# Key and probability transposes moved from PE to DVE's 32x32 blocks, with 512-column output projections, in a one-core decode kernel

## The chip, the cores and the metric

The kernel runs on one core of a Trainium2 chip. A core has five engines that run side by side and meet through semaphores: PE (matrix products), DVE (vector), ACT (activations), POOL, and SP, which here only issues transfers. Data moves from HBM into SBUF (128 partitions) by 16 DMA engines; PE writes into PSUM, 8 banks of 512 words per partition, and DVE or ACT read it out.

The metric is the device time of the program in microseconds: the median of 3 runs before is 231.6 us (231.56 to 231.65).

## The reference

One decode step for two batch rows: layer norm of x, grouped-query attention over the last 4096 positions of a cache (32 query heads, 8 key heads of 128 channels), and a gated MLP, both added to x.

```python
W = min(4096, max(256, Sk // 4))                      # 4096
q = (x @ wq).reshape(B, Sq, Hq, Dh).transpose(0, 2, 1, 3)
k = jnp.repeat(k_cache[:, :, Sk - W:, :], rep, axis=1)
v = jnp.repeat(v_cache[:, :, Sk - W:, :], rep, axis=1)
p = _softmax(jnp.einsum("bhqd,bhkd->bhqk", q, k) * (Dh ** -0.5))
o = jnp.einsum("bhqk,bhkd->bhqd", p, v)               # ... @ wo
...
gate = xn @ W_gate; gate = gate * (gate > 0)
mlp = (gate * (xn @ W_up)) @ W_down
return x + attention(xn) + mlp                        # all float32
```

## The kernel before

**Tiles.** The 16 (batch row, key head) pairs are worked on in `NG` = 4 groups `g`, each one batch row and `C` = 4 key heads, and each group in `NP` = 2 steps `a` of two heads. A step loads one key tile and later one value tile of [128, 8192] words (4 MiB): partition `2 * pk + h` holds 64 successive positions of head `h` of the two. All big loads (wq in two, w_gate, w_up, 8 key tiles, 8 value tiles, w_down, wo in two) go through one pool `ring` of four buffers and one queue, SP's, in program order. A load can be issued when the buffer four loads back has been read for the last time; SP stands at it until then, and so do the loads behind it.

**Keys.** The scores need keys with channels on the partitions. In `transposes` (L305 to L316) PE turns a key tile 128x128 at a time into a PSUM bank `pk`, and DVE and ACT by turns copy each bank into `kT`, separating the two heads. `kT` (two buffers) holds half a tile (`s1` = 0 or 1), 2 heads of 2048 positions. `scores` (L329) multiplies it with `qz`, in which each head's four queries stand in columns of their own: 8 products of 512 columns per half, whose outputs go to the four groups `32 * q` of 32 rows of the bank `s`.

**Softmax.** `softmax` takes the maxima over each row (`m`), turns them (`mt`), joins the rows of one query (`mx`, `mb`), turns them back (`nm`), and one ACT instruction writes the exponentials `p`, each twice. PE turns `p` in 8 pieces (`pp`), and DVE copies with a mask `own` into `pt`.

**Values.** `values` multiplies `pt` with a value tile, 16 products on four row groups of `o`; `o` is copied to `on`, and `gather` adds up the parts that belong to a head into `oa` by four small products. `finish` divides by the sums, `spread_heads` puts the heads where wo needs them (`oT`).

**Order.** The kernel is written with a manual schedule: each engine executes in the order of the program text. `kwork` weaves: the generator `softmax(g - 1)` is advanced by one piece after each bank of transposes of group `g`, and the scores of a half tile follow the transposes of the next half. `values` of group `g - 1` come after the transposes of the same step of `g`.

**Ends.** Ahead of the loop stand the norm, q (`q_ps`, `qt`, `qz`) and the MLP's two products (`g_ps`, `u_ps`, `x_ps`, `ht_ps`). Behind it `project` multiplies each of the 49 rows of 512 of w_down and wo in four products of 128 columns (`y_ps`, 17 output rows on each of the four groups); wo's second half is loaded in parts of 8, 5, 2 and 1 of its 16 rows, and the output leaves when the last part has been used.

Of the kernel before, what the change touches and what calls it, by code (L numbers as in the profile page):

```python
# [20 lines left out]
def kernel(  # L21
# [28 lines left out]
    S1 = W // (Q * 512)  # L50

# [10 lines left out]
    ps_kt = ctx.enter_context(tc.tile_pool(name="ps_kt", bufs=3, space=PSUM))  # L62
# [77 lines left out]

    NSLOT = C * S1
# [21 lines left out]
    for e in range(NE):  # L163
# [3 lines left out]
    pick = const.tile([P, 4, 24], F32, name="pick")  # L167
    nc.gpsimd.memset(pick, 0.0)
    nc.vector.tensor_reduce(
        out=pick[:, :, 8:16], in_=ident.rearrange("p (q u k) -> p u k q", q=Q, u=4), op=ALU.add, axis=AX.X  # L170
    )


    HK = 2 * REP
    by_h = const.tile([P, NP, HK], F32, name="by_h")
    nc.vector.tensor_reduce(
        out=by_h, in_=ident.rearrange("p (q a s k) -> p a k q s", q=Q, a=NP, s=S1), op=ALU.add, axis=AX.XY
    )

    half_of = const.tile([P, 2], F32, name="half_of")  # L180
    nc.vector.tensor_reduce(
        out=half_of, in_=ident.rearrange("p (y h) -> p h y", h=2), op=ALU.add, axis=AX.X
    )
    own = const.tile([P, 2, REP], F32, name="own")
    nc.vector.tensor_copy(own, half_of[:, :, None].to_broadcast([P, 2, REP]))
# [42 lines left out]
    for r in range(R):  # L228
        qs = work.tile([P, 512], F32, name=f"qs{r}", tag="qs")
        (nc.vector.tensor_copy if r else nc.scalar.copy)(qs, q_ps[r])  # L230
        qt = ps_kt.tile([P, REP, C, 16, B], F32, name=f"qt{r}", tag="kt")
        for i in range(REP):
            nc.tensor.transpose(
                qt[:, i].rearrange("p c s b -> p (c s b)"), qs[:, i * P:(i + 1) * P], ident
            )
        for b in range(B):
            dst = qz[:, r * B + b].rearrange("p (a s h k) -> p a s h k", a=NP, s=S1, h=2)
            for h in range(2):
                nc.vector.tensor_copy(
                    dst[:, :, :, h, 0:REP], qt[:, :, h::2, 0:S1, b].rearrange("p i a s -> p a s i")  # L240
                )
# [4 lines left out]
    x_ps = ps_1.tile([32, 2, FX], F32, name="x_ps", tag="o0")  # L246
# [36 lines left out]
    ht_ps = ps_1.tile([P, FM + SX, B], F32, name="ht_ps", tag="misc")  # L283
    for k in range(FM):
        for c in range(Q):
            nc.tensor.matmul(
                ht_ps[32 * c:32 * c + 32, k], hh[:, k], ident[:, 32 * c:32 * c + B], start=True, stop=True
            )
    for k in range(SX):
        m = 64 if k < RX else 32  # L290
        nc.tensor.matmul(ht_ps[0:m, FM + k], hx[:, k, 0:m], ident[0:32, 0:B], start=True, stop=True)
    nc.vector.tensor_copy(hT[:, 0:FM, :, 0], ht_ps[:, 0:FM])
    nc.vector.tensor_copy(hT[0:64, FM:FM + RX, :, 0], ht_ps[0:64, FM:FM + RX])
    if LEFT:
        nc.vector.tensor_copy(hT[0:32, FM + RX, :, 0], ht_ps[0:32, FM + RX])

    HW = W // S1
    ss, pts, rls = {}, {}, {}  # L300
    kts, osb = {}, {}
    turn = [0]

    def evacuate(dst, src):
        (nc.vector.tensor_copy if turn[0] % 2 else nc.scalar.copy)(dst, src)  # L305
        turn[0] += 1

    def transposes(g, a, s1, kt_in):

        kt = ktp.tile([P, 2, HW], F32, name=f"kT{g}_{a}_{s1}", tag="kT")  # L310
        kts[g, a, s1] = kt
        for n in range(2 * Q):
            pk = ps_kt.tile([P, 512], F32, name=f"pk{g}_{a}_{s1}_{n}", tag="kt")
            for u in range(4):
                j = 8 * Q * s1 + 4 * n + u
                nc.tensor.transpose(pk[:, u * P:(u + 1) * P], kt_in[:, j * P:(j + 1) * P], ident)  # L316
            evacuate(
                kt[:, :, n * 256:(n + 1) * 256], pk.rearrange("p (y h) -> p h y", h=2),
            )
            yield  # L320

    def scores(g, a, s1):
        if (a, s1) == (0, 0):
            ss[g] = ps_s.tile([P, 512], F32, name=f"s{g}", tag="s")
        kt = kts.pop((g, a, s1))
        for h in range(2):
            n = (a * S1 + s1) * 2 + h
            for q in range(Q):
                nc.tensor.matmul(  # L329
                    ss[g][32 * q:32 * q + 32, :], qz[:, g, 32 * n:32 * n + 32],  # L330
                    kt[:, h, q * 512:(q + 1) * 512],
                    start=(a == 0 and s1 == 0 and h == 0), stop=(a == NP - 1 and s1 == S1 - 1 and h == 1),
                )

    def softmax(g):
# [3 lines left out]
        yield  # L339
        mt = ps_1.tile([1, P], F32, name=f"mt{g}", tag="misc")  # L340
        nc.tensor.transpose(mt, m, ident)
        mx = work.tile([1, NP, HK], F32, name=f"mx{g}", tag="mx")
        nc.vector.tensor_reduce(
            out=mx, in_=mt.rearrange("p (q a s k) -> p a k q s", q=Q, a=NP, s=S1), op=ALU.max, axis=AX.XY
        )
        mb = work.tile([1, NP, S1, HK], F32, name=f"mb{g}", tag="mb")
        nc.vector.tensor_scalar(
            mb, mx[:, :, None, :].to_broadcast([1, NP, S1, HK]), -SCALE, None, op0=ALU.mult
        )
        yield  # L350
        nm_ps = ps_1.tile([P, 1], F32, name=f"nm_ps{g}", tag="misc")
        for q in range(Q):
            nc.tensor.matmul(
                nm_ps[32 * q:32 * q + 32, :], mb.rearrange("p a s k -> p (a s k)"), ones, start=True, stop=True
            )
        nm = work.tile([P, 1], F32, name=f"nm{g}", tag="nm")
        nc.vector.tensor_copy(nm, nm_ps)  # L357

        p = work.tile([P, 512, 2], F32, name=f"p{g}", tag="p", bufs=1)
        l = work.tile([P, 1], F32, name=f"l{g}", tag="l")  # L360
        both = ss[g][:, :, None].to_broadcast([P, 512, 2])
        nc.scalar.activation(p, both, AF.Exp, bias=nm, scale=SCALE, accum_out=l)  # L362
        yield
        yield
        yield

        pts[g] = work.tile([P, 2, Q * NP * S1, 4, HK], F32, name=f"pt{g}", tag="pt")
        pv = p.rearrange("r y h -> r (y h)")
        for jh in range(2):
            pp = ps_kt.tile([P, 4, P], F32, name=f"pp{g}_{jh}", tag="kt")  # L370
            for u in range(4):
                lo = (4 * jh + u) * P
                nc.tensor.transpose(pp[:, u], pv[:, lo:lo + P], ident)  # L373
            nc.vector.tensor_tensor(  # L374
                pts[g][:, jh].rearrange("p n u k -> p u n k"), pp.rearrange("p u (n k) -> p u n k", k=HK),
# [56 lines left out]
    def kwork(g, a, kt_in, others=()):  # L432
# [11 lines left out]
        for o in others:  # L444
            for _ in o:
                pass
# [85 lines left out]
```

## Time and profile before

| | |
|---|---|
| median of 3 runs | 231.60 us |
| the profiled execution | 231.43 us, of which its span is 229.6 us |
| PE busy | 185.4 us (mean granted clock 0.938) |
| DVE busy | 67.2 us |
| ACT busy | 46.9 us |
| DMA | 94.90 MB read, queue busy 96.7% of the span |

The span runs from the first instruction of the program on the core to the last; what lies around it, 1.8 us here, is start and end of the execution. Busy times of PE are of pipelined products and overlap; a line `x256` counts records, two for each float32 product. In the groups of instructions the first number behind the bar is the busy time of all, then the mean duration of one in ns, then the idle time before them and who ended it. In the windows PEclk is the granted PE clock as a share of the full one, and the DMA share is the mean busy share of the 16 DMA engines.

### The profile page before, as it was taken

The numbers are of one execution on the slowest core, as the hardware profiler recorded it, in microseconds if no ns is written. First come the engines' busy times: TensorE is split into PE (matmuls) and PEld (weight loads), VectorE is DVE, ScalarE is ACT, GpSimd is POOL, SyncE is SP. The second block draws the span as 40 slices with busy tenths as digits, with TensorE's granted clock in tenths as the row PEclk, the third lists the DMA queues.
The fourth block names the chain that finished last, engine by engine and source line by source line (L and its number), as shares of the span: only waits on it lengthen the run. The fifth ranks groups of instructions, "written<-read, shape, count | busy, mean of one in ns | idle before, by whom it ended". The sixth has DMA issues, their size and how long they took to land.

```text
span 229.6 us, 4149 instructions
## 1 busy us (share of the span) xinstructions
PE 185.4 (81%) x1876; PEld 114.7 (50%) x1876; DVE 67.2 (29%) x135; ACT 46.9 (20%) x80; POOL 8.2 (4%) x25
## 2 busy tenths in 40 slices
PE   0059961779999899997799699889979973988794
PEld 0052231259666583663484566458446532247682
DVE  0320021034444570441472143157124224001000
ACT  0020100004344451440351233045023202010000
POOL 8100000000000000000000000000000300000000
PEclk9999999577999999999999799999999999599678
DMA  7999999999999999999999999999999999999981
GB/s 274 451 428 408 454 410 437 422 451 442 405 425 451 415 417 445 442 411 420 457 417 432 428 440 414 434 445 414 422 440 437 417 428 440 423 442 414 410 364 49
DMA packets 3824, 95.15 MB, mean 414 GB/s; under 512 B 434, under 2 KB 448, under 8 KB 704
## 3 DMA queue, kind: packets, MB, share of 16 engines
q1 hardware_dynamic: 3796, 94.90, 96.7%
q8 instruction: 14, 0.23, 0.4%
q14 instruction: 2, 0.02, 0.0%
q10 hardware_dynamic: 12, 0.00, 0.0%
HBM read 94.90 MB, written 0.00 MB: 413 GB/s over the span
## 4 chain that ended last, share of the span: by engine, by line
DMA 54%; PE 41%; DVE 2%; issue 1%; ACT 1%; ACTq 0%; POOL 0%; DVEq 0%
DMA k<-in_A_k_cache_dram 37%; PE pk L316 21%; DMA wo<-in_A_wo_dram 13%; PE s L329 7%; PE y_ps L480 5%; DMA x<-in_A_x_dram 4%; PE o L393 3%; PE q_ps L222 3%; PE xt_ps L212 2%; ACT p L362 1%; PE pp L373 0%; ACTq L135 0%; PE oa L409 0%; DVE stats L189 0%; DVE kT L305 0%
## 5 line engine op out<-in xcount | busy, mean ns | idle before, releaser
L316 PE MATMUL pk<-ident,k 128*128 128x128 f32 x512 | 67.9, 286 | 6.0 <-DMA k<-in_A_k_cache_dram 5.9
L316 PEld LDWEIGHTS pk<-ident,k 128*128 128x128 f32 x512 | 57.9, 146 | 20.9 <-issue 16.7
L305 DVE COPY kT<-pk 128x512 f32<-128x512 f32 x64 | 44.2, 691 | 52.1 <-PE pk L316 46.2
L305 ACT COPY kT<-pk 128x512 f32<-128x512 f32 x64 | 37.5, 585 | 69.5 <-PE pk L316 69.5
L393 PE MATMUL o<-v,pt 128*32 128x512 f32 x256 | 32.5, 641 | 0.0
L329 PE MATMUL s<-kT,qz 128*32 128x512 f32 x256 | 30.9, 598 | 0.0
L393 PEld LDWEIGHTS o<-v,pt 128*32 128x32 f32 x256 | 11.3, 117 | 15.7 <-issue 10.9
L212 PE MATMUL xt_ps<-rep,xn 2*128 2x32 f32 x16 | 3.7, 400 | 13.9 <-DVE xn L206 13.9
L329 PEld LDWEIGHTS s<-kT,qz 128*32 128x32 f32 x256 | 7.1, 109 | 11.9 <-issue 11.5
L305 DVE COPY on<-o 128x512 f32<-128x512 f32 x4 | 2.8, 692 | 30.5 <-PE o L393 30.5
L409 PE MATMUL oa<-on,pick 128*16 128x128 f32 x64 | 8.3, 273 | 4.1 <-DVE on L305 3.3
L480 PE MATMUL y_ps<-wo,oT 128*17 128x128 f32 x256 | 10.3, 329 | 1.6 <-DMA wo<-in_A_wo_dram 1.6
L409 PEld LDWEIGHTS oa<-on,pick 128*16 128x16 f32 x64 | 5.8, 97 | 11.3 <-DVE on L305 7.0
L250 PE MATMUL u_ps<-wu,xnT 128*32 128x416 f32 x32 | 5.8, 901 | 6.1 <-DMA wu<-in_B_W_up_dram 6.1
L212 PEld LDWEIGHTS xt_ps<-rep,xn 2*128 2x128 f32 x16 | 3.6, 320 | 13.9 <-issue 13.9
L222 PE MATMUL q_ps<-wq,xnT 128*32 128x512 f32 x64 | 9.7, 777 | 0.5 <-DVE xnT L214 0.5
L480 PEld LDWEIGHTS y_ps<-wo,oT 128*17 128x17 f32 x256 | 8.1, 119 | 3.6 <-DMA wo<-in_A_wo_dram 2.6
L305 ACT COPY on<-o 128x512 f32<-128x512 f32 x4 | 2.3, 586 | 27.0 <-PE o L393 27.0
L98 POOL MEMSET wx<- 64x2048 f32 x1 | 1.8, 1804 | 169.1 <-PE s L329 169.1
L362 ACT ACTIVATE p<-s,nm 128x1024 f32<-128x1024 f32 x4 | 4.5, 1114 | 13.1 <-DVE nm L357 13.1
L374 DVE TENSOR_TENSOR pt<-pp,own 128x512 f32<-128x512 f32 x8 | 5.4, 689 | 2.6 <-PE pp L373 2.6
L373 PE MATMUL pp<-ident,p 128*128 128x128 f32 x32 | 4.9, 280 | 1.7 <-ACT p L362 1.5
(83 smaller groups left out, 68.2 us busy)
## 6 DMA issues: line engine op xcount, KB each, us to landing
k<-in_A_k_cache_dram SPq DMA_DIRECT2D x8, 4096.0 KB, 23.9
v<-in_A_v_cache_dram SPq DMA_DIRECT2D x8, 4096.0 KB, 28.3
wq<-in_A_wq_dram SPq DMA_DIRECT2D x2, 4096.0 KB, 21.7
wo<-in_A_wo_dram SPq DMA_DIRECT2D x1, 4096.0 KB
wg<-in_B_W_gate_dram SPq DMA_DIRECT2D x1, 3584.0 KB, 29.8
wu<-in_B_W_up_dram SPq DMA_DIRECT2D x1, 3584.0 KB, 39.3
wd<-in_B_W_down_dram SPq DMA_DIRECT2D x1, 3328.0 KB
wo<-in_A_wo_dram SPq DMA_DIRECT2D x1, 2048.0 KB
```

The source lines that it names most:

```text
L212: nc.tensor.matmul(xt_ps[:, o, kc, :], cols, rep.rearrange("r s b -> r (s b)"), start=True, stop=True)
L222: nc.tensor.matmul(q_ps[r][32 * c:32 * c + 32, :], xnT[:, 0, kc, :], wqt[kc // 2][:, kc % 2, n * 512:(n + 1) * 512], start=(kc == 0), stop ...
L250: nc.tensor.matmul(dst[32 * c:32 * c + 32, :], xnT[:, 1, kc, :], wt[:, kc, c * MQ:(c + 1) * MQ], start=(kc == 0), stop=(kc == KC - 1),)
L305: (nc.vector.tensor_copy if turn[0] % 2 else nc.scalar.copy)(dst, src)
L316: nc.tensor.transpose(pk[:, u * P:(u + 1) * P], kt_in[:, j * P:(j + 1) * P], ident)
L329: nc.tensor.matmul(ss[g][32 * q:32 * q + 32, :], qz[:, g, 32 * n:32 * n + 32], kt[:, h, q * 512:(q + 1) * 512], start=(a == 0 and s1 == 0 ...
L362: nc.scalar.activation(p, both, AF.Exp, bias=nm, scale=SCALE, accum_out=l)
L373: nc.tensor.transpose(pp[:, u], pv[:, lo:lo + P], ident)
L374: nc.vector.tensor_tensor(pts[g][:, jh].rearrange("p n u k -> p u n k"), pp.rearrange("p u (n k) -> p u n k", k=HK), own.rearrange("p h i ...
L393: nc.tensor.matmul(o[32 * q:32 * q + 32, :], pts[g][:, jh, n].rearrange("p u k -> p (u k)"), v[:, lo:lo + 512], start=(s1 == 0 and jh == 0 ...
L409: nc.tensor.matmul(oa[g], pick[:, u, 8 - 8 * a:24 - 8 * a], ons[a][:, u], start=(a == 0 and u == 0), stop=(a == NP - 1 and u == 3),)
L480: nc.tensor.matmul(y_ps[32 * e:32 * e + 17, :], lhsT.rearrange("p b s -> p (b s)")[:, 0:17], w[:, e * P:(e + 1) * P], start=False, stop=stop,)
```

## The change

The key tile is no longer turned by PE. DVE's transpose turns each 32x32 block by itself, so channels `32 * c` to `32 * c + 31` of 32 partitions (16 runs of positions, two heads) land on 32 partitions; `kT` becomes [128, 4 channel blocks, 2 heads, 32 positions, 16 runs], and `qz` block diagonal: partition group `pb` holds q for its own positions only, with q copied to the four partition groups by products with `spot`. The two heads of a key tile are now `a` and `a + 2`.

```diff
@@ load_kv
-        base = cache[b, r * C + 2 * a, SK - W:SK, :]
+        base = cache[b, r * C + a, SK - W:SK, :]
-            tensor=cache.tensor, offset=base.offset, ap=[[run, PK], [SK * DH, 2], [1, run]]
+            tensor=cache.tensor, offset=base.offset, ap=[[run, PK], [NP * SK * DH, 2], [1, run]]
@@ set-up
-    qz = const.tile([P, NG, NSLOT * 36], F32, name="qz")
+    ZW = 3 * 16
+    qz = const.tile([P, NG, CB, 2, ZW], F32, name="qz")
     nc.gpsimd.memset(qz, 0.0)
+    spot = const.tile([P, CB, PB, L], F32, name="spot")
+    nc.gpsimd.tensor_copy(
+        spot, ident.rearrange("p (c e) -> p c e", c=CB)[:, :, None, :].to_broadcast([P, CB, PB, L])
+    )
...
+    perm = const.tile([P, 2, P], F32, name="perm")
+    nc.gpsimd.memset(perm, 0.0)
...
@@ q
+        qT = work.tile([P, B, C, REP], F32, name=f"qT{r}", tag="qT")
+        nc.vector.tensor_copy(qT, qt[:, :, :, 0, :].rearrange("p i c b -> p b c i"))
+        rq = ps_1.tile([P, CB, B, C, REP], F32, name=f"rq{r}", tag="misc")
+        for cb in range(CB):
+            nc.tensor.matmul(
+                rq[:, cb].rearrange("p b c i -> p (b c i)"), spot[:, cb].rearrange("p b e -> p (b e)"),
+                qT.rearrange("p b c i -> p (b c i)"), start=True, stop=True,
+            )
...
@@ keys
-            for u in range(4):
-                j = 8 * Q * s1 + 4 * n + u
-                nc.tensor.transpose(pk[:, u * P:(u + 1) * P], kt_in[:, j * P:(j + 1) * P], ident)
-            evacuate(
-                kt[:, :, n * 256:(n + 1) * 256], pk.rearrange("p (y h) -> p h y", h=2),
-            )
...
+        for s1 in range(S1):
+            kt = ktp.tile([P, CB, 2, JH, KL], F32, name=f"kT{g}_{a}_{s1}", tag="kT")
+            for n in range(2):
+                lo = JH // 2 * n
+                j = JH * s1 + lo
+                nc.vector.transpose(
+                    kt[:, :, :, lo:lo + JH // 2, :].rearrange("p c h j k -> p j c k h"),
+                    kt_in[:, j * DH:(j + JH // 2) * DH],
                 )
+            for cb in range(CB):
+                for h in range(2):
+                    lo = 32 * (2 * s1 + h)
+                    nc.tensor.matmul(
+                        ss[g][lo:lo + 32, :], qz[:, g, cb, h, 16 * a:16 * a + 32],
+                        kt[:, cb, h].rearrange("p j k -> p (j k)"),
+                        start=(a == 0 and cb == 0), stop=(a == NP - 1 and cb == CB - 1),
+                    )
```

The softmax keeps its steps, but writes each exponential once. `turn` permutes its rows by two products with `perm` and turns the result with one DVE transpose; the mask moves behind the value products, and `gather` is one product per step followed by a sum over `u` on DVE.

```diff
+    def turn(g, p, l):
+        pp = ps_kt.tile([P, 2, 512], F32, name=f"pp{g}", tag="kt")
+        for h in range(2):
+            nc.tensor.matmul(pp[:, h], perm[:, h], p, start=True, stop=True)
+        pts[g] = work.tile([P, NP * S1, JH, HK], F32, name=f"pt{g}", tag="pt")
+        nc.vector.transpose(pts[g].rearrange("p n j k -> p j n k"), pp.rearrange("p h y -> p y h"))
...
@@ values, gather, finish
-        evacuate(ons[a].rearrange("p u d -> p (u d)"), o)
+        nc.vector.tensor_tensor(
+            ons[a], o.rearrange("p (u d) -> p u d", u=4), mask[:, :, None].to_broadcast([P, 4, P]), op=ALU.mult
+        )
...
-        for u in range(4):
-            nc.tensor.matmul(
-                oa[g], pick[:, u, 8 - 8 * a:24 - 8 * a], ons[a][:, u],
-                start=(a == 0 and u == 0), stop=(a == NP - 1 and u == 3),
-            )
+        nc.tensor.matmul(
+            oa[g], picks[:, a].rearrange("p h a i -> p (h a i)"), ons[a], start=(a == 0), stop=(a == NP - 1)
+        )
...
+        su = work.tile([HR, P], F32, name=f"su{g}", tag="su", bufs=1)
+        nc.vector.tensor_reduce(out=su, in_=oa[g].rearrange("h u d -> h d u"), op=ALU.add, axis=AX.X)
+        nc.vector.tensor_scalar(osb[r][:, b], su, rls[g], None, op0=ALU.mult)
@@ the loop
+    for g in range(NG):
+        for a in range(NP):
             kt_in = load_kv(k_cache, "k", g, a)
+            v_in = load_kv(v_cache, "v", g - 1, a) if g else None
+            scores(g, a, kt_in)
+            nm = maxima(g) if a else None
+            if g:
+                values(g - 1, a, v_in)
+            pl = softmax(g, nm) if a else None
+            if g:
+                gather(g - 1, a)
+                if a:
+                    finish(g - 1)
+                elif g % B == 1 and g > 1:
+                    spread_heads((g - 2) // B)
             if a:
...
+                turn(g, *pl)
```

At the end the rows of w_down and the first 24 of wo are each one product of 512 columns into one of four row groups of `y4`; `y4` is copied and folded into `y_ps` by four products, and the last 8 rows of wo stay products of 128 columns.

```diff
+    def slot(lhsT, w):
+        t, i = done[0] % Q, done[0]
+        nc.tensor.matmul(
+            y4[32 * t:32 * t + 32, :], lhsT.rearrange("p b s -> p (b s)"), w, start=(i < Q), stop=(i >= EARLY - Q)
+        )
+        done[0] += 1
...
+            if (r, j) < (1, cuts[1][1]):
+                slot(oT[:, r, j], wt[:, j])
+                continue
+            if j == cuts[1][1]:
+                ys = work.tile([P, D], F32, name="ys", tag="qs")
+                nc.vector.tensor_copy(ys, y4)
+                quarters(fold[:, 0:17], ys, False)
+            quarters(oT[:, r, j].rearrange("p b s -> p (b s)")[:, 0:17], wt[:, j], (r, j) == (R - 1, NJ - 1))
```

The order on DVE moves. Before, in the second step of group 2 and the start of group 3 (`kT_1_0` and `kT_1_1` are the two halves of the step's key tile, `on_1` the copy of the value product of group 1, `kT_0_0` the first half of group 3):

```order
L305 COPY kT_1_0_1052<-pk_1_0_6_1089 128x2x256
L305 COPY kT_1_1_1109<-pk_1_1_0_1110 128x2x256
L305 COPY kT_1_1_1109<-pk_1_1_2_1122 128x2x256
L305 COPY kT_1_1_1109<-pk_1_1_4_1134 128x2x256
L305 COPY kT_1_1_1109<-pk_1_1_6_1146 128x2x256
L305 COPY on_1_1188<-o_1_1171 128x512
L418 TENSOR_SCALAR osb_873<-oa_1166,rl_994 16x128
L305 COPY kT_0_0_1199<-pk_0_0_1_1206 128x2x256
L338 TENSOR_REDUCE m_1226<-s_1020 128x1
L305 COPY kT_0_0_1199<-pk_0_0_3_1228 128x2x256
L343 TENSOR_REDUCE mx_1236<-mt_1234 1x16
```

Now DVE in the same step of group 2:

```order
L337 STREAM_TRANSPOSE kT_1_0_591<-k_1_587 128x16x4x16x2 x2
L337 STREAM_TRANSPOSE kT_1_1_602<-k_1_587 128x16x4x16x2 x2
L353 TENSOR_REDUCE m_613<-s_543 128x1
L357 TENSOR_REDUCE mx_617<-mt_615 1x16
L362 TENSOR_SCALAR mb_619<-mx_617 1x64 x2
L368 COPY nm_624<-nm_ps_622 128x1
L400 TENSOR_TENSOR on_1_643<-o_1_626,mask 128x512
L417 TENSOR_REDUCE su_649<-oa_585 16x128
L418 TENSOR_SCALAR osb_526<-su_649,rl_537 16x128
L382 STREAM_TRANSPOSE pt_655<-pp_652 128x32x4x8
L386 RECIPROCAL rl_659<-lp_657 16x1
L337 STREAM_TRANSPOSE kT_0_0_666<-k_0_661 128x16x4x16x2 x2
```

The maxima of a group stood among the next group's key copies; they now stand, with the value product's mask and the turning of `p`, between the transposes of one key tile and those of the next.

PE in the same step before, from the value products of group 1 to the first transposes and maxima of group 3's start:

```order
L329 MATMUL s_1020<-kT_1_0_1052,qz 32x512 x8
L409 MATMUL oa_1166<-on_0_1046,pick 16x128 x4
L393 MATMUL o_1_1171<-v_1_1050,pt_954 32x512 x16
L409 MATMUL oa_1166<-on_1_1188,pick 16x128 x4
L316 MATMUL pk_0_0_0_1200<-ident,k_0_1195 128x128 x4
L316 MATMUL pk_0_0_1_1206<-ident,k_0_1195 128x128 x4
L329 MATMUL s_1020<-kT_1_1_1109,qz 32x512 x8
L316 MATMUL pk_0_0_2_1220<-ident,k_0_1195 128x128 x4
```

and now:

```order
L344 MATMUL s_543<-kT_1_0_591,qz 32x512 x8
L344 MATMUL s_543<-kT_1_1_602,qz 32x512 x8
L355 MATMUL mt_615<-ident,m_613 1x128
L366 MATMUL nm_ps_622<-ones,mb_619 128x1
L395 MATMUL o_1_626<-v_1_589,pt_533 32x512 x16
L408 MATMUL oa_585<-on_1_643,picks 16x512
L380 MATMUL pp_652<-p_645,perm 128x512 x2
L384 MATMUL lp_657<-l_646,by_h 16x1
L344 MATMUL s_665<-kT_0_0_666,qz 32x512 x8
```

Scores used to be followed by transposes of the next tile; now nothing of the next tile stands on PE until its own scores.

More of the change, by code (lines that the diff above doesn't have):

```diff
@@ L50 @@
     S1 = W // (Q * 512)
+    L = 32
+    PB = P // L
+    CB = DH // L
     NP = C // 2
@@ L364, in softmax @@
[L364 to L370, printed above, removed]
-            for u in range(4):
[L372 to L375, printed above, removed]
-                own.rearrange("p h i -> p (h i)")[:, None, None, :].to_broadcast([P, 4, Q * NP * S1, HK]), op=ALU.mult,
-            )
-            yield
+        nc.scalar.activation(p, ss[g], AF.Exp, bias=nm, scale=SCALE, accum_out=l)
```

184 lines of the change are left out of this document (69 added, 115 removed).

## The prediction

> **What bounds the kernel now.** I began with the page: busy times, the slices, the chain of waits.
>
> ```profile
> span 229.6 us, 4149 instructions
> PE 185.4 (81%) x1876; PEld 114.7 (50%) x1876; DVE 67.2 (29%) x135; ACT 46.9 (20%) x80; POOL 8.2 (4%) x25
> DMA  7999999999999999999999999999999999999981
> HBM read 94.90 MB, written 0.00 MB: 413 GB/s over the span
> DMA 54%; PE 41%; DVE 2%; issue 1%; ACT 1%; ACTq 0%; POOL 0%; DVEq 0%
> ```
>
> PE looks like the bound at 81%, but the transfers are busy in every slice between the first and the last two. The view by windows, over one batch-and-row group each, says the same:
>
> ```profile
> core 0: us, PE busy (x) PEld busy (x) DVE busy (x) ACT busy (x) POOL busy (x), PEclk, DMA share, GB/s
> 90.00:129.00 39.00, 34.49 (x303) 20.73 (x294) 14.65 (x25) 11.64 (x20) 0.00 (x0) 1.00 1.00 429
> 129.00:168.00 39.00, 37.12 (x307) 24.18 (x307) 14.86 (x26) 10.47 (x18) 0.00 (x0) 0.96 1.00 430
> ```
>
> A group moves four 4 MiB tiles (16.78 MB); at 430 GB/s that is **39.0 us**. As long as compute turns a group round in 39 us, it is hidden. How much lateness the ring of four buffers forgives shows in the chain of waits:
>
> ```profile
> 24.50 26.72 DMA k<-in_A_k_cache_dram
> 100.73 28.26 DMA k<-in_A_k_cache_dram
> ```
>
> The first key tile lands at 51.22. A later one is issued 28 us before it lands, and its transfer alone takes some 10: compute may slip by about 15 us once, not in every group. The kernel is bound by HBM.
>
> **The change: the transposes.** 512 PE transposes and 128 copies go. Instead DVE runs 32 transposes, two per half tile, each of 2048 elements per partition, 8 per group. No such operation stands in the trace, so its duration T is bounded by DVE rows:
>
> ```profile
> L305 DVE COPY kT<-pk 128x512 f32<-128x512 f32 x64 | 44.2, 691 | 52.1 <-PE pk L316 46.2 <-ACT on L305 5.2
> L357 DVE COPY nm<-nm_ps 128x1 f32<-128x1 f32 x4 | 0.6, 158 | 1.8 <-PE nm_ps L353 1.8
> L206 DVE TENSOR_SCALAR xn<-xc,rs 2x512 f32<-2x512 f32 x1 | 0.5, 474 | 0.0
> L261 DVE SCALAR_TENSOR_TENSOR gr<-gs 128x416 f32<-128x416 f32 x1 | 0.6, 592 | 4.5 <-ACT gs L259 4.5
> L263 DVE TENSOR_TENSOR hh<-gr,u_ps 128x416 f32<-128x416 f32 x1 | 0.9, 872 | 11.6 <-PE u_ps L250 11.6
> L374 DVE TENSOR_TENSOR pt<-pp,own 128x512 f32<-128x512 f32 x8 | 5.4, 689 | 2.6 <-PE pp L373 2.6
> ```
>
> - One element at a time: (691 - 158)/511 = 1.043 ns each, so T = 0.158 + 2047 x 1.043 ns = **2.29 us**.
> - As fast as the quickest SBUF-to-SBUF row (xn): (474 - 158)/511 = 0.62 ns, T = 1.43 us. The lower end.
> - gr and hh both handle 416 elements. hh writes each element 32 words from the last and takes 280 ns more: 0.67 ns per element. pt writes runs of 8 neighbours and pays nothing over kT. The new kT write alternates: head 0, head 1, head 0, 512 words (2 KB) apart, so no two successive elements are neighbours. With hh's surcharge: 1.043 + 0.673 = 1.716 ns, T = **3.67 us**.
> - Twice the one-element rate, as if a 4-byte word took two passes: T = 4.43 us. The upper end.
>
> I take 3.67: of these rows, hh has the write pattern that this transpose has. The Trainium skill, Vector Engine (DVE) Microarchitecture Reference, section 5.2, has 1.71 ns per column for a destination that hops 4 KiB at every element, which hh's row here bears out. Its section 3.8 says the transpose front-end sustains one element per cycle per lane; by that alone T would be 2.29 and the sum below 231.1. No row here shows a transpose; that case is a rival.
>
> **Scores.** Each half tile still takes 8 products of 512 columns, but its output rows are now `32 * (2 * s1 + h)`: two groups of 32 PE columns where there were four.
>
> ```profile
> L329 PE MATMUL s<-kT,qz 128*32 128x512 f32 x256 | 30.9, 598 | 0.0
> L255 PE MATMUL x_ps<-wg,xnT 128*32 128x128 f32 x8 | 1.0, 272 | 0.0
> 123.44 3.62 PE L393 MATMUL o<-v,pt 128*32 128x512 f32 x32
> 195.47 6.37 PE L393 MATMUL o<-v,pt 128*32 128x512 f32 x32
> ```
>
> On four groups a 512-column record costs 30.9/256 = 0.12 us. x_ps stays in one group: 8 records of 128 columns in 1.0 us less a pipeline of 0.2 is 0.11 each, so 0.44 per 512 columns. The four groups thus overlap nearly fully, and two give 0.22 per record: 16 records, **3.6 us**, where 1.9 were (the bounds). `o` keeps four groups: 3.62. The second o row is one at half clock: 6.37.
>
> **The chain.** The old order wove softmax and copies between transposes. Now DVE runs in program order: 4 transposes, then it stands at `on` until PE has done the last scores and 16 value products; the next tile's transposes are queued behind it. So these times add. In the second tile of a group the maxima, the head sum and `turn` join. Rows for them:
>
> ```profile
> L338 DVE TENSOR_REDUCE m<-s 128x1 f32<-128x512 f32 x4 | 2.8, 691 | 4.8 <-PE s L329 4.8
> L341 PE MATMUL mt<-ident,m 128*1 128x128 f32 x4 | 1.1, 272 | 0.8 <-DVE m L338 0.8
> L343 DVE TENSOR_REDUCE mx<-mt 1x16 f32<-1x128 f32 x4 | 1.1, 272 | 0.4 <-PE mt L341 0.4
> L347 DVE TENSOR_SCALAR mb<-mx 1x32 f32<-1x32 f32 x4 | 0.7, 169 | 0.1
> L353 PE MATMUL nm_ps<-ones,mb 1*32 1x1 f32 x32 | 1.0, 172 | 2.8 <-DVE mb L347 2.8
> L362 ACT ACTIVATE p<-s,nm 128x1024 f32<-128x1024 f32 x4 | 4.5, 1114 | 13.1 <-DVE nm L357 13.1
> L382 DVE RECIPROCAL rl<-lp 16x1 f32<-16x1 f32 x4 | 0.6, 146 | 0.0
> ```
>
> - Maxima: 0.69 + 0.27 + 0.27 + 0.22 (two mb, overlapping) + 0.24 (nm_ps, 1.0 over four groups) + 0.16 = 1.85.
> - `oa`, one full-width product of 512 columns (two records of 0.44): 0.9. `pp`, two of them: 1.8; the sum over u and osb run beside it. `pt`, 1024 elements in runs of 8: 0.158 + 1.07 = 1.23. `rl`: 0.15.
> - exp has half the columns of L362, about 0.7, beside `o`.
>
> First tile: 4T + 3.6 + 3.62 + 0.69 = 4T + 7.9. Second: 4T + 3.6 + 1.85 + 3.62 + 0.69 + 0.9 + 1.8 + 1.23 + 0.15 = 4T + 13.8. Some 13 handoffs at 0.06 (s ends at 112.60, m starts at 112.67 in the timeline's two rows below): 0.8.
>
> ```profile
> 110.68 1.92 PE L329 MATMUL s<-kT,qz 128*32 128x512 f32 x16
> 112.67 0.69 DVE L338 TENSOR_REDUCE m<-s 128x1 f32<-128x512 f32 x1 [1.14 <-PE s L329]
> ```
>
> **A group costs 8T + 22.5.** At T = 3.67 that is 51.9 us against the transfers' 39.0: the bound moves to the DVE-PE chain, late by 13 us per group, more than the ring forgives. What is late next is the queue: a key buffer is freed after its transposes, so SP's load stands until then, and DMA gets gaps.
>
> Group 0 has no values: 51.2 + 8T + 3.6 + 1.85 + 0.7 (exp) + 1.8 (pp) + 1.4 (pt, rl) + 0.6 (handoffs) = 61.2 + 8T. Three groups: 24T + 67.5. The tail after the last `pt`:
>
> ```profile
> 212.74 1.97 PE L423 MATMUL op<-osb,spread 16*128 16x32 f32 x16
> L480 PE MATMUL y_ps<-wd,hT 128*17 128x128 f32 x104 | 3.2, 273 | 0.0
> L502 DVE COPY yo<-y_ps 128x128 f32<-128x128 f32 x1 | 0.3, 291 | 11.7 <-PE y_ps L480 11.7
> 227.00 0.60 SPq L503 DMA_DIRECT2D out_dram<-yo  x1
> ```
>
> Two rounds of o, on, oa (10.4), 17 slots of w_down at two records of 0.12 (4.1), op and oT (2.2), 24 slots of wo (5.8), copying y4 and folding it (0.9), 8 rows in quarters at eight records of 3.2/104 = 0.031 (2.0), yo 0.3, output to the span's end 2.6, handoffs 0.8: **29.1**. Wider products save nothing: 0.24 a row against 0.25. The last wo rows land some 18 us after `pt` (two queued tiles of about 10 us, the first issued a little before it); PE asks for them at 24.
>
> Span = 61.2 + 24T + 8T + 67.5 + 29.1 = **157.8 + 32T**, but never below the transfers' 229.6. At T = 3.67: 275.2. The profiled execution took 231.43 for its 229.6, 0.2 us under the median of 231.6; with 1.8 outside the span: **277 us**.
>
> **Costed at nothing.** More set-up on POOL (a wider qz, spot, picks, perm, at most some 4 us):
>
> ```profile
> 11.75 0.55 POOL L195 TENSOR_TENSOR sd<-ve,half 2x1 f32<-2x1 f32 x1 [5.15 <-DVE ve L193]
> 41.53 5.78 PE L250 MATMUL u_ps<-wu,xnT 128*32 128x416 f32 x32 [6.14 <-DMA wu<-in_B_W_up_dram]
> ```
>
> POOL idles 5.15 us ahead of sd. Without that cover q slips by what is over, and the first key load, issued at 24.5, waits in the queue behind wu until about 41 anyway. The longer q path (rq) hides in PE's 6.14 us before wu; uncovered it costs about 1.5 us.
>
> **PE's clock.** With PE idle for 2T at the start of each tile it will be cold:
>
> ```profile
> 125.93:129.34 3.41, 1.34 (x14) 0.38 (x7) 0.00 (x0) 0.58 (x1) 0.00 (x0) 1.00 1.02 432
> 129.34:132.76 3.42, 3.42 (x18) 3.42 (x17) 1.38 (x2) 0.73 (x2) 0.00 (x0) 0.50 0.96 412
> 132.76:136.17 3.41, 3.41 (x32) 1.87 (x30) 1.38 (x2) 1.61 (x3) 0.00 (x0) 1.00 1.01 432
> ```
>
> A window with 1.34 us of work is followed by one at 0.50, and a full one restores 1.00. The first scores of a tile would then take up to 7.2 us, inside 2T = 7.3: hidden. Were `o` cold too, 2.7 us more in each tile that has values: up to 8 x 2.7 = 22.
>
> **The rivals.**
> - A, one element per cycle (T = 2.29). For: the contiguous rows. Against: hh. The formula gives a span of 231.1, 232.9 us, but 2T = 4.6 no longer hides cold scores: up to 7.2 - 4.6 = 2.6 late in a tile, about half of that where the clock comes back in their midst, and less where the queue is ahead: 233 to 244, about 239 us. Slower still. Chance 0.17. The Trainium skill's rule of one element per cycle (Vector Engine (DVE) Microarchitecture Reference, section 3.8) would make it this case; no row shows it.
> - B, on the other side: transposes at or under 2.24 us with PE warm. From 157.8 + 32T = 229.6 the point is T = 2.24; below it the chain fits within the transfers and the time is theirs, 231.6, give or take 0.8. xn's 0.62 ns is for it, the alternating write against it. Chance 0.08; nothing in the profile favours either sign within it.
> - C, two passes (T = 4.43): 157.8 + 141.8 + 1.8 = 301 us. Only the missing row is for it. Chance 0.10.
>
> **Numbers.** Forecast (T between 3.3 and 4.1, 266 to 290 us): 0.65. Leaving out B, the quickest of A, and C: 236 to 292, about 0.8. A run of this kernel can tell 0.2% from nothing; B splits into faster 0.03, same 0.03, slower 0.02; so faster 0.03, same 0.03, slower 0.94.
>
> **What would show it.** A transpose row near 3.7 us, DVE about 145 us busy (117 of it transposes), scores at 3.6 us per half tile, DMA slices below 9 from group 1 on, SP's loads waiting for DVE. It is wrong if transposes take 2.3 us, if DMA stays full, or if PE's cold clock puts o on 6 us throughout.

## The result, and the profile after

The changed kernel is slower: a median of 281.56 us (6 runs, 278.70 to 282.69) against 231.48 us (6 runs, 231.28 to 231.65) for the kernel before. The ratio is 1.2148, with a 95% interval of 1.2093 to 1.2203. The profiled execution took 278.70 us, for a span of 276.9.

The page of the changed kernel: the span, the busy times, then the busy share of DVE, the granted clock and the transfers in 40 slices, and the shares of the chain that ended last, by engine and by line.

```profile
span 276.9 us, 2272 instructions
PE 169.2 (61%) x976; PEld 54.7 (20%) x976; DVE 148.1 (53%) x125; ACT 8.6 (3%) x28; POOL 10.2 (4%) x33
DVE  1300324699952992794379639824990497240201
PEclk9999869559897759959995797799659958999999
DMA  7999999999999906997995299799907992989930
HBM read 94.90 MB, written 0.00 MB: 343 GB/s over the span
DVE 47%; PE 35%; DMA 13%; issue 3%; ACT 0%; ACTq 0%; POOL 0%; DVEq 0%
```

Before, the transfers filled every slice and headed the chain with 54%. Now they have holes (a 0 and a 6 in slices 15 and 16, then one hole or more per group), the rate is 343 GB/s where it was 413, and DVE and PE share the chain. The bytes are the same: nothing is loaded twice, loads are issued later. Who makes them late stands in the waits of SP's queue (total us, times, longest), before and now:

```profile
SPq L70 <- PE pk L316: 83.3, 8, 13.3
```

```profile
SPq L73 <- DVE kT L337: 120.3, 7, 25.4
```

Before, too, a load stood behind the transposes that read its buffer, 83 us in all, and the transfers had no hole. Now it is 120 us, and the longest wait is 25.4 us where it was 13.3. The groups of instructions give the prices (busy us and mean ns behind the bar, then the idle time before them):

```profile
L337 DVE STREAM_TRANSPOSE kT<-k 128x2048 f32<-128x2048 f32 x32 | 115.8, 3728 | 2.3 <-DMA k<-in_A_k_cache_dram 2.3
L344 PE MATMUL s<-kT,qz 128*32 128x512 f32 x256 | 76.9, 757 | 69.1 <-DVE kT L337 69.1
L382 DVE STREAM_TRANSPOSE pt<-pp 128x1024 f32<-128x1024 f32 x4 | 5.0, 1250 | 7.0 <-PE pp L380 7.0
```

One transpose of a quarter key tile takes 3.73 us, and PE idles 69 us for them. Whether the two take turns is seen in the chain of waits (start, duration, engine, tile, line, count); here is group 1, from one group's first transposes to the next's, and a piece of group 3:

```profile
91.26 14.41 DVE kT L337 x4
105.71 2.34 PE s L344 x10
...
109.34 3.46 PE o L395 x26
...
113.43 14.51 DVE kT L337 x4
...
127.98 3.65 PE s L344 x16
...
131.65 0.70 DVE m L353
...
133.80 3.62 PE o L395 x32
...
138.18 1.03 PE oa L408 x2
139.22 1.93 PE pp L380 x4
...
141.17 1.25 DVE pt L382
...
142.46 14.41 DVE kT L337 x4
...
215.95 1.03 PE oa L408 x2
216.98 1.91 PE op L423 x16
```

Read it downwards: DVE for 14.4 us, PE for 7, DVE for 14.5, then a dozen shorter steps by turns (not all are shown), and the next tile's transposes only behind them. From 91.26 to 142.46 a group takes 51.2 us, 12 more than its transfers need. Four transposes in 14.41 us mean 3.60 to 3.63 for each, some 0.1 under the mean of a single row: successive ones overlap a little.

### The profile page after: what moved, and what is told of

Its sections match the earlier page's. It is cut to its first block, busy times and chain, and to the rows that moved or that the text cites. A ratio compares the mean times of both kernels' runs of the same rounds, so it can differ in the third digit from the quotient of the medians.

```text
span 276.9 us, 2272 instructions
## 1 busy us (share of the span) xinstructions
PE 169.2 (61%) x976; PEld 54.7 (20%) x976; DVE 148.1 (53%) x125; ACT 8.6 (3%) x28; POOL 10.2 (4%) x33
## 4 chain that ended last, share of the span: by engine, by line
DVE 47%; PE 35%; DMA 13%; issue 3%; ACT 0%; ACTq 0%; POOL 0%; DVEq 0%
DVE kT L337 40%; PE o L395 10%; DMA k<-in_A_k_cache_dram 10%; PE s L344 9%; PE y L467 4%; PE pp L380 3%; DMA x<-in_A_x_dram 3%; PE oa L408 2%; PE q_ps L240 2%; DVE pt L382 2%; DVE on L400 2%; PE op L423 1%; PE xt_ps L230 1%; DVE m L353 1%; PE y_ps L474 1%
## 5 line engine op out<-in xcount | busy, mean ns | idle before, releaser
L344 PE MATMUL s<-kT,qz 128*32 128x512 f32 x256 | 76.9, 757 | 69.1 <-DVE kT L337 69.1
L337 DVE STREAM_TRANSPOSE kT<-k 128x2048 f32<-128x2048 f32 x32 | 115.8, 3728 | 2.3 <-DMA k<-in_A_k_cache_dram 2.3
L344 PEld LDWEIGHTS s<-kT,qz 128*32 128x32 f32 x256 | 16.5, 134 | 125.4 <-DVE kT L337 80.5
L400 DVE TENSOR_TENSOR on<-o,mask 128x512 f32<-128x512 f32 x8 | 5.5, 692 | 40.4 <-PE o L395 40.4
L408 PE MATMUL oa<-on,picks 128*16 128x512 f32 x16 | 8.3, 597 | 6.5 <-DVE on L400 6.5
L380 PE MATMUL pp<-p,perm 128*128 128x512 f32 x16 | 9.2, 703 | 1.2 <-ACT p L374 1.2
L382 DVE STREAM_TRANSPOSE pt<-pp 128x1024 f32<-128x1024 f32 x4 | 5.0, 1250 | 7.0 <-PE pp L380 7.0
L267 DVE COPY qz<-rq 32x32 f32<-32x32 f32 x16 | 3.0, 187 | 7.1 <-ACT qz L267 7.1
L467 PE MATMUL y<-wo,oT 128*32 128x512 f32 x48 | 5.4, 594 | 0.0
L467 PE MATMUL y<-wd,hT 128*32 128x512 f32 x26 | 4.5, 595 | 0.0
```

What stands on the lines that cost most here:

```text
L267: (nc.vector.tensor_copy if a else nc.scalar.copy)(qz[rows, r * B + b, :, :, lo:lo + REP], rq[rows, :, b, a::NP, :])
L337: nc.vector.transpose(kt[:, :, :, lo:lo + JH // 2, :].rearrange("p c h j k -> p j c k h"), kt_in[:, j * DH:(j + JH // 2) * DH],)
L344: nc.tensor.matmul(ss[g][lo:lo + 32, :], qz[:, g, cb, h, 16 * a:16 * a + 32], kt[:, cb, h].rearrange("p j k -> p (j k)"), start=(a == 0 an ...
L380: nc.tensor.matmul(pp[:, h], perm[:, h], p, start=True, stop=True)
L382: nc.vector.transpose(pts[g].rearrange("p n j k -> p j n k"), pp.rearrange("p h y -> p y h"))
L400: nc.vector.tensor_tensor(ons[a], o.rearrange("p (u d) -> p u d", u=4), mask[:, :, None].to_broadcast([P, 4, P]), op=ALU.mult)
```

## The experiments

The theory: two properties of the change make it slow. The transposes write with a hop of 2 KB at every element, and the order makes DVE and PE take turns. The first three kernels mend one of the two each, the next two take PE's share in it, and the last four the end of the kernel and the repairs together. Medians of the kernel before on the same chips were 231.24 to 231.29 us.

**Runs of 16 neighbours.** One change in the order of the write. What a column of `kT` holds is then mixed between heads and positions; the amount of work stays the same.

```diff
-                    kt[:, :, :, lo:lo + JH // 2, :].rearrange("p c h j k -> p j c k h"),
+                    kt[:, :, :, lo:lo + JH // 2, :].rearrange("p c h j k -> p j c h k"),
```

> The changed kernel, but each key transpose writes runs of 16 neighbouring words instead of alternating between two heads 2 KB apart; kT then holds keys of both heads mixed, so the scores are not the reference's; all sizes and counts are the same. Theory (the alternating write costs 0.67 ns per element, the transpose itself runs at one element per 1.04 ns): the transpose row falls from 3.73 to about 2.3 us (pitch 3.62 to 2.2), and the span by 32 x 1.4 = 45 us to 231.5, plus up to 1.4 us of cold scores in each of 8 tiles: 232 to 243 us. Rival (a transpose of 4-byte words out of SBUF costs 1.7 ns per element wherever it writes): row stays 3.7, time 279 to 283.

Measured: 240.28 us (one run), a span of 238.5. The groups of instructions of this kernel:

```profile
L337 DVE STREAM_TRANSPOSE kT<-k 128x2048 f32<-128x2048 f32 x32 | 71.0, 2272 | 3.9 <-DMA k<-in_A_k_cache_dram 2.4 <-PE s L344 1.5
```

Down from 3728 to 2272 ns: 1.11 ns for each of 2048 elements in place of 1.82. The alternating write alone cost 0.71 ns per element, and 41 of the 50 us by which the change is slower go with it. The quick price is the prediction's rival A (2.29 us), whose 239 us came out at 240.3.

**The same, with scores that are right.** The two heads alternate inside `kT`, so that the transpose writes 32 neighbours in a row, and PE reads its moving operand at a step of two words.

```diff
-            kt = ktp.tile([P, CB, 2, JH, KL], F32, name=f"kT{g}_{a}_{s1}", tag="kT")
+            kt = ktp.tile([P, CB, JH, KL, 2], F32, name=f"kT{g}_{a}_{s1}", tag="kT")
...
-                    kt[:, :, :, lo:lo + JH // 2, :].rearrange("p c h j k -> p j c k h"),
+                    kt[:, :, lo:lo + JH // 2].rearrange("p c j k h -> p j c k h"),
...
-                        kt[:, cb, h].rearrange("p j k -> p (j k)"),
+                        kt[:, cb, :, :, h].rearrange("p j k -> p (j k)"),
```

> The changed kernel with the two heads innermost in kT, so that a transpose writes 32 neighbouring words, and PE reads each head's keys in steps of two words; the result is the reference's. Theory: transposes as in the run with runs of 16 (about 2.3 us). If PE reads steps of two words at its full rate, time 232 to 245 us. Rival (PE's moving operand slows down at a step of two words): scores of a half tile take about 7.2 us instead of 3.63, PE becomes the bound within a tile, two half tiles 14.4 + o 3.6 + handoffs, 255 to 275 us.

Measured: 240.63 us (4 runs, 240.28 to 243.28), 1.0431 times the kernel before (1.0375 to 1.0487). From its page, the chain that ended last by engine, and two groups of instructions:

```profile
PE 58%; DVE 22%; DMA 15%; issue 3%; ACT 0%; ACTq 0%; POOL 0%; DVEq 0%
...
L344 PE MATMUL s<-kT,qz 128*32 128x512 f32 x256 | 65.7, 731 | 38.6 <-DVE kT L337 38.6
L337 DVE STREAM_TRANSPOSE kT<-k 128x2048 f32<-128x2048 f32 x32 | 71.0, 2272 | 3.9 <-DMA k<-in_A_k_cache_dram 2.3 <-PE s L344 1.6
```

Runs of 32 cost what runs of 16 do, and the scores take 65.7 us as in the kernel above (65.6). PE reads every second word at nearly the same rate: the 32 records of a tile's scores, after the same 3.38 us of idling, take 8.18 us against 8.04. But the repair is not whole. The chain has gone over to PE, from 35% to 58%, and the time stays 9 us over the kernel before.

**The order alone.** The alternating write stays. The transposes become a function of their own; those of the next tile's first half are written right behind the scores, those of its second half behind the softmax, ahead of `gather`, `finish` and `turn`. The maxima move behind the value products.

```diff
+    kt_in = load_kv(k_cache, "k", 0, 0)
+    kts = [keys(0, 0, s1, kt_in) for s1 in range(S1)]
...
-            scores(g, a, kt_in)
-            nm = maxima(g) if a else None
+            scores(g, a, kts)
+            gn, an = divmod(NP * g + a + 1, NP)
+            if gn < NG:
+                kt_in = load_kv(k_cache, "k", gn, an)
+                kts = [keys(gn, an, 0, kt_in)]
...
+            nm = maxima(g) if a else None
             pl = softmax(g, nm) if a else None
+            if gn < NG:
+                kts.append(keys(gn, an, 1, kt_in))
```

> The changed kernel with the same instructions in another order: the two transposes of each half of the next key tile are written ahead of on and of turn, so that DVE works on the next tile while PE does the last scores and the value products. Theory (what makes the group slow is that 8T and 22.5 us of PE round trips add up): T stays 3.7, but a group costs DVE's own 8 x 3.62 + about 6 = 35 us, less than the 39 us of its transfers, so the kernel is bound by HBM again: 231 to 238 us. Rival (DVE's or PE's own throughput is the bound, and order does not matter): at least 265 us.

Measured: 232.59 us (4 runs, 232.07 to 232.85), 1.0054 times the kernel before (1.0037 to 1.0070). From its page, the span, DVE and the transfers by slices, and the group of the transposes:

```profile
span 230.9 us, 2278 instructions
DVE  2120032259999997899998999998999804312001
DMA  7999999999999999999999999999999999999970
...
L334 DVE STREAM_TRANSPOSE kT<-k 128x2048 f32<-128x2048 f32 x32 | 117.6, 3773 | 2.9 <-DMA k<-in_A_k_cache_dram 1.8 <-PE s L347 1.1
```

The transposes are as slow as in the changed kernel, DVE is as busy (147.6 us), and yet 49 of the 50 us are gone. DVE's slices are now nearly full from slice 10 to 31 and the transfers have no hole. They are only just ahead: the chain that ended last still runs through DVE for 42% of the span and through transfers for 23%. The timeline shows DVE turning keys while PE multiplies:

```profile
93.90 5.12 PE L347 MATMUL s<-kT,qz 128*32 128x512 f32 x25
...
96.30 1.21 DVE L385 STREAM_TRANSPOSE pt<-pp 128x1024 f32<-128x1024 f32 x1
...
98.60 7.49 DVE L334 STREAM_TRANSPOSE kT<-k 128x2048 f32<-128x2048 f32 x2 [1.07 <-PE s L347]
...
99.74 4.00 PE L398 MATMUL o<-v,pt 128*32 128x512 f32 x26
```

So the two repairs overlap: 41 and 49 us, of 50 in all. Slow transposes count mostly because PE's work stands in line with them, and the line counts mostly because the transposes are slow. Neither is the whole: with runs of 32 the line still costs 9.5 us (240.63 against 231.09 us, the last kernel below). Either repair brings a group near its 39 us of transfers, and below that there is little to gain.

**Scores on four column groups.** The prediction charged 1.7 us per half tile for two groups in place of four. Here both halves of a tile add into the same four groups of rows, so the scores are sums of two halves.

```diff
-                    lo = 32 * (2 * s1 + h)
+                    lo = 32 * (2 * (cb % 2) + h)
...
-                        start=(a == 0 and cb == 0), stop=(a == NP - 1 and cb == CB - 1),
+                        start=(a == 0 and s1 == 0 and cb < 2), stop=(a == NP - 1 and s1 == S1 - 1 and cb >= 2),
```

> The changed kernel with the scores of a half tile spread over four groups of 32 output rows by the channel block's parity instead of two; both halves' scores add up in the same rows, so the result is not the reference's; all sizes and counts are the same. Theory (two groups overlap half as well as four): 16 records of a half tile fall from 3.63 to about 1.9 us, 8 tiles save 1.7 us each, 14 us in all: 263 to 268 us. Rival (the score product is limited by something else, its operands or weight loads): no change, 278 to 283 us.

Measured: 287.41 us (one run), slower than the changed kernel by more than its runs differ among themselves. Theory and rival both missed. The page's clock by slices, then the timeline of one tile:

```profile
PEclk9999669667755578655675795558667755599999
```

```profile
128.50 3.64 PE L344 MATMUL s<-kT,qz 128*32 128x512 f32 x16 [3.57 <-DVE kT L337]
...
134.59 6.38 PE L395 MATMUL o<-v,pt 128*32 128x512 f32 x32
```

And the view by windows over these two, whose columns are those of the prediction's windows:

```profile
128.50:132.14 3.64, 3.64 (x16) 0.59 (x16) 0.00 (x0) 0.00 (x0) 0.00 (x0) 0.50 0.80 288
134.59:140.97 6.38, 6.38 (x33) 1.39 (x32) 0.16 (x1) 0.78 (x2) 0.00 (x0) 0.56 0.76 329
```

The mean clock is 0.731, against 0.852. The last scores of this tile need 3.64 us, as long as on two groups in the changed kernel, and the value products 6.38 where they took 3.62. Both ran at about half the clock, 0.50 and 0.56. The scores do so throughout: the 16 records take 3.35 to 3.64 us in each of the 16 half tiles. The reading is that PE now works too little to be granted the full clock; it idles 3.57 us ahead of these scores, where it was 1.61. To tell this from four groups that are simply no faster, PE got the missing work back.

**Four groups, the first half's products twice.** Each product of a tile's first half is issued twice, so the scores count that half double.

```diff
-            for cb in range(CB):
+            for i, cb in enumerate(list(range(CB)) * (2 if s1 == 0 else 1)):
...
-                        start=(a == 0 and s1 == 0 and cb < 2), stop=(a == NP - 1 and s1 == S1 - 1 and cb >= 2),
+                        start=(a == 0 and s1 == 0 and i < 2), stop=(a == NP - 1 and s1 == S1 - 1 and cb >= 2),
```

> The kernel of b_groups (four groups for the scores) with the products of each tile's first half issued twice, so that PE has as much to do under the second half's transposes as the changed kernel has; the result is not the reference's. Theory (four groups halve the last scores, but b_groups left PE too idle for its clock to come back): the clock comes back in each tile as in the changed kernel, the last scores take 1.9 us and o 3.6, 14 us less than the changed kernel's 277: span 262 to 268, time 264 to 270. Rival (four groups bring nothing even at full clock, or the clock was not what made b_groups slow): 278 to 288.

Measured: 267.78 us (one run), clock 0.852. Its timeline, in the same tile:

```profile
116.18 5.98 PE L344 MATMUL s<-kT,qz 128*32 128x512 f32 x32 [6.17 <-DVE kT L337]
123.52 1.92 PE L344 MATMUL s<-kT,qz 128*32 128x512 f32 x16 [1.36 <-DVE kT L337]
```

and the window of the last scores:

```profile
123.52:125.44 1.92, 1.92 (x16) 0.42 (x16) 0.00 (x0) 0.00 (x0) 0.00 (x0) 1.00 0.85 256
```

Twice the work in the first half, and the kernel is 20 us quicker than the one above. The last scores now run at the full clock and take 1.92 us, in this tile and in the seven others, so four groups do halve them: the 1.7 us per half tile of the sum was right, and the clock had hidden it. (The value products of this one tile still take 5.34 us; those of the others take 3.6.)

**The end alone, and the end undone.** Two kernels ask what the wide products of w_down and wo are worth: the reordered kernel with the end of the kernel before (`project`, four products of 128 columns per row), and the kernel before with the changed end (`slot`, `y4`, `fold`). The core of the first edit, which the second makes the other way round:

```diff
-            if (r, j) < (1, cuts[1][1]):
-                slot(oT[:, r, j], wt[:, j])
-                continue
...
-            quarters(oT[:, r, j].rearrange("p b s -> p (b s)")[:, 0:17], wt[:, j], (r, j) == (R - 1, NJ - 1))
+            project(oT[:, r, j], wt[:, j], (r, j) == (R - 1, NJ - 1))
```

> c_order with the old end: every row of w_down and wo in four products of 128 columns, no y4 and no fold. Theory (in c_order 1.1 us more than before is left at the end: copying y4, folding it and 8 rows behind it stand after the last landing): 231.4 to 232.0, at least 0.5 us under c_order's 232.6. Rival (the wide products are worth something at the end, or the rest is earlier): 232.6 or more.

> The kernel before with the changed end alone: 512-column products of w_down and 24 rows of wo into y4, its copy, the fold and 8 rows of 128-column products; nothing else changed. Theory (a wide row costs PE 0.24 us against 0.25, and copy and fold come after): 231.9 to 232.9, 0.4 to 1.4 us slower than before. Rival (fewer products let PE be done earlier): 230.8 to 231.4.

Measured: the reordered kernel with the old end 233.14 us (6 runs, 231.85 to 233.43), 1.0068 times the kernel before (1.0048 to 1.0088), so not below the 232.59 of the wide end. The kernel before with the wide end 231.03 us (11 runs, 230.77 to 231.18), ratio 0.9989 (0.9980 to 0.9997). Both theories fall, and both times lie in their rivals' ranges: the wide end does not cost the reordered kernel its last microsecond, and in the kernel before it gains about 0.2 us. In the kernel before with the wide end, the timeline shows PE pausing for wo:

```profile
216.05 3.64 PE L489 MATMUL y<-wo,oT 128*32 128x512 f32 x32 [0.56 <-DMA wo<-in_A_wo_dram]
221.04 1.92 PE L489 MATMUL y<-wo,oT 128*32 128x512 f32 x16 [1.35 <-DMA wo<-in_A_wo_dram]
```

The transfers bound the end of the kernel before with either width: the load of wo has 13% of the chain that ended last there, and 8% with the wide end.

**Both repairs.** If the end's products are not to blame for the last microsecond, late loads may be: slow transposes free a key buffer later even where DVE works without a pause. The reordered kernel with the old end, and now with the layout of runs of 32:

```diff
-        kt = ktp.tile([P, CB, 2, JH, KL], F32, name=f"kT{g}_{a}_{s1}", tag="kT")
+        kt = ktp.tile([P, CB, JH, KL, 2], F32, name=f"kT{g}_{a}_{s1}", tag="kT")
...
```

> c_order with the old end (as d_tail) and with the heads innermost in kT (as f_stride). Theory (HBM is the bound in both): transposes at 2.27 instead of 3.77 us bring nothing any more, the same as d_tail within 0.4 us: 231.0 to 232.0. Rival (slow transposes still delay loads or the end): at least 0.6 us under d_tail.

Measured: 230.85 us (12 runs, 230.69 to 232.47), ratio 0.9989 (0.9977 to 1.0000), and 2.3 us under its neighbour with slow transposes, so the theory missed and the rival is met. The timelines of the two, first with slow and then with quick transposes: the issue of wo's last half, and the last copy before the output.

```profile
206.10 1.75 SPq L490 DMA_DIRECT2D wo<-in_A_wo_dram  x4
...
228.43 0.29 DVE L494 COPY yo<-y_ps 128x128 f32<-128x128 f32 x1 [9.26 <-PE y_ps L472]
```

```profile
200.87 1.76 SPq L490 DMA_DIRECT2D wo<-in_A_wo_dram  x4
...
226.07 0.29 DVE L494 COPY yo<-y_ps 128x128 f32<-128x128 f32 x1 [12.13 <-PE y_ps L472]
```

The load is issued 5.2 us sooner and the end comes 2.4 us sooner. The shares of the chain that ended last, in the same order:

```profile
DVE 42%; PE 27%; DMA 23%; issue 5%; ACT 1%; ACTq 0%; POOL 0%; DVEq 0%
```

```profile
DMA 66%; DVE 16%; PE 16%; issue 0%; ACTq 0%; POOL 0%; DVEq 0%
```

With quick transposes the chain runs through the loads, that of wo among them. With slow ones no load of wo stands in it: it runs through the transposes to the last `pt`, which ends at 201.8 us against 196.6, and on through PE, with a pause of 1.65 us in the products of wo for which the profile names no cause. So it is the slow transposes that cost the last 2.3 us. Whether they do so by the late load or by the late last group is not shown: the load waits for that group's value products, and both come 5.2 us later.

**Both repairs and the wide end.** The same three lines of layout in the reordered kernel:

```diff
...
-                        kt[:, cb, h].rearrange("p j k -> p (j k)"),
+                        kt[:, cb, :, :, h].rearrange("p j k -> p (j k)"),
...
```

> c_order with the heads innermost in kT (as f_stride) and the wide end: the changed kernel with its two costs mended, the alternating write and the serial order. Theory (HBM is the bound; the wide end gave 0.2 us in h_wide): like g_best or up to 0.4 us under it, 230.4 to 231.0, 0.1 to 0.4% under before. Rival (behind a DVE-turned key tile PE's clock is cold at the end, and the copy and fold of y4 come late as in c_order): 231.2 to 232.6.

Measured: 231.09 us (12 runs, 230.69 to 231.66), ratio 0.9991 (0.9982 to 1.0000), between the theory's range and the rival's. Three kernels end within 0.3 us of each other and some 0.1% under the kernel before, at the edge of what can be told. With the chain mended this kernel is bound by the same transfers as before (66% of its chain), and PE's 512 transposes, which the change took away, had been hidden under them.

| kernel | us | ratio to before |
|---|---|---|
| changed | 281.56 | 1.2148 |
| runs of 16 in the write | 240.28 | one run |
| runs of 32, PE at a step of two | 240.63 | 1.0431 |
| order alone | 232.59 | 1.0054 |
| four column groups | 287.41 | one run |
| four groups, first half twice | 267.78 | one run |
| order, old end | 233.14 | 1.0068 |
| before, wide end | 231.03 | 0.9989 |
| order, runs of 32, old end | 230.85 | 0.9989 |
| order, runs of 32, wide end | 231.09 | 0.9991 |

## Why the prediction was right

The forecast was 277 us (span 275.2); the profiled execution took 278.7 (span 276.9), the median is 281.56. Both the mechanism, a chain of DVE and PE in place of the transfers, and its main price held.

- **T, the duration of a transpose.** Predicted 3.67 us from the surcharge in `hh`'s row; measured 3.73, at 3.62 from one start to the next. Both halves of that reasoning were confirmed apart: without the hop the transpose takes 2.27 us, near the 2.29 of one element at a time. The Trainium skill, Vector Engine (DVE) Microarchitecture Reference, sections 3.8 and 5.2, gives one element per cycle for the transpose and 1.71 ns per column for a destination that hops 4 KiB at every element. The runs agree with the first where the write is in runs (2272 ns for 2048 elements is 1.11 ns each, and 1.03 without the prediction's fixed 0.158 us); where it hops they lie 2 to 6% over the second (1.82 ns, and 1.74 without it).
- **Scores.** Predicted 3.6 us per half tile, measured 3.63 to 3.65; four groups take 1.92. The working's 0.11 us for a record of `x_ps` is 0.10 by the figures it gives ((1.0 - 0.2) / 8), which would have made it 3.2; the runs bear out the 0.11.
- **The first half cold (at half the clock), and hidden.** The timeline of the changed kernel, the first and the last half of a tile's scores:

```profile
120.77 5.59 PE L344 MATMUL s<-kT,qz 128*32 128x512 f32 x16 [6.17 <-DVE kT L337]
127.98 3.63 PE L344 MATMUL s<-kT,qz 128*32 128x512 f32 x16 [1.61 <-DVE kT L337]
```

The half after 6.17 us of idling takes 5.59 us, and PE still waits 1.61 for the next transposes: no time lost, as costed. That PE is warm for the second half and for `o` hangs on the sizes: with less work in the first half it was not, in the kernel on four groups. The prediction had named a cold `o` as its danger.
- **A group.** Predicted 51.9, measured 51.2 twice. The third took 54.4 (from 193.66 to the last `pt`'s end at 248.0). Here a term was missing: `spread_heads` for the first groups stands in group 3 ahead of the next transposes, which brings `oa` (1.03 us) and `op` (1.91) into the chain above, with a copy and handoffs around them. The prediction counted it in the tail alone. That the span came out within 1.7 us is in part luck: two groups at 0.7 us less than predicted take back more than half of what the third costs more.
- **Group 0 and the tail.** The first `pt` ended at 91.2 (predicted 90.6): the set-up stayed hidden, the first key tile landing at 50.8 (predicted 51.2), but `pp` found PE cold and took 3.24 us against 1.8. The tail took 28.9 (predicted 29.1). The 15 us by which compute was said to be free to slip once is 18 by the figures given there (28 less 10); no term uses it.
- **Rival A.** Its 239 us were nearly met when the write was mended, but its place was only partly right. The formula with 2.29 gives a span of 231.1, and the measured one is 238.5. In the kernel with runs of 16 a regular group takes 41.7 us (81.52 to 123.20, by its transposes), of which the value products are a part:

```profile
112.85 5.34 PE L395 MATMUL o<-v,pt 128*32 128x512 f32 x32
```

This cold `o` costs 1.7 over its 3.62; rival A had expected the loss in the first scores. In the third group (44.7 us) the missing `spread_heads` adds some 3, and the first `pt` ends 2.0 us later than the formula has it. The chain has another form, too: in a tile it runs through two transposes (4.5 us) and then both halves of the scores (8.0), 12.5 in all, where the formula has four transposes and one half, 12.8. That the number was near is in part luck.
- **What the sum had no term for.** The profiled execution was the quickest of six, and the median is 2.9 us over it. The kernel before spreads by 0.16%, the changed one by 1.4%. Its runs do not order by mean clock (281.27 us at 0.823, 280.75 at 0.859), so the cause is open; that the clock steps fall at other places of a tile from run to run is only argued.

## What to carry to other kernels

When work moves to an engine that writes its output in a pattern of its own, price the write: look for the innermost step of the destination, and have it run over neighbours even if the reader then steps (here two words, at some 2% of the scores' time). And before an operation is moved off a busy engine, ask which engine was the bound: PE at 81% was not, so taking its transposes away could not gain, while the new order lost the overlap. In a kernel whose engines take turns, write the next tile's first stage ahead of this tile's last steps; that edit alone took back 49 of 50 us here.

## What the runs showed of the hardware

- Less work made the kernel slower. Spreading the scores over four groups, which at full clock halves their time, took the changed kernel from 281.56 to 287.41 us at a granted clock of 0.731, and products issued twice brought it to 267.78 at 0.852. The Trainium skill, TensorE: Matmul & The Clock Gate, section "What's actually happening", has the clock halved after an idle window of about 3.4 us; the four-group run agrees in its sizes, with an idle gap of 3.57 us ahead of its slow scores. The window need not be empty of work, however: in the kernel before, 3.41 us with 1.34 us of work in them were followed by 0.50 (the prediction's windows).
- PE reads a moving operand with a step of two words within 2% of the speed of a contiguous one: 8.18 against 8.04 us for the 32 records of a tile, 65.7 against 65.6 us busy for all 256.
- A transpose of 2048 elements takes 2272 ns with runs of 16 as of 32 in its write, 3728 ns when it alternates between two places 2 KB apart, although each place for itself is written in order.
